# A second table of biases and engine choices for the planner of a fused FFT and SwiGLU kernel

## The chip, the cores and the metric

The kernel runs on one core of a Trainium2 chip. A core has a matrix engine (TensorE, PE in the profile; PEld is its weight load), a vector engine (VectorE, DVE), an engine for activation functions (ScalarE, ACT), a general engine (GpSimd, POOL) and a queue that only issues DMAs (SyncE, SP). The engines run side by side, each works off its own instructions in a fixed order, and they meet at semaphores. The metric is the device time of one execution in microseconds (us). The kernel before takes 603.48 us, the median of three runs (603.24, 603.48 and 603.62).

## The reference

```python
def _attn_ref(x):                       # x: 8 x 3008 x 256, float32
    X = np.fft.fft(x, axis=1)
    X = np.fft.fft(X, axis=2)
    return X.real.astype(np.float32)

def _moe_ref(x, w_gate, w_val, w_out):  # 24064 x 256, d_ff = 1536
    g = x @ w_gate
    silu = g * (1.0 / (1.0 + np.exp(-g)))
    val = x @ w_val
    return (silu * val @ w_out).astype(np.float32)
```

The real part of a two-dimensional Fourier transform of each of the 8 batches goes, row by row, through a gated feed-forward block of hidden width 1536.

## The kernel before

The transform has mirror symmetry. Only half of the 3008 rows of a batch are transformed, into an even part P and an odd part Q (tiles Pt and Qt, transposed, so that rows are columns). The feature transform is folded into the weights: Wp belongs to P, Wq to Q, and Wm is Wq with the signs of the mirrored row. From one column of P and Q come a plus row and a minus row of the output.

The 12,032 half rows are cut into 24 tiles of 512 columns, but for tiles 0 and 3 (480 columns) and tile 23 (320). Each tile has 12 blocks of 128 hidden features; one block of one tile is a unit, so there are 288 units. A unit forms two gates in one PSUM tile g and two values in one PSUM tile v. There are three buffers each for g and v, and two for o, the PSUM tiles of the output products. A unit goes like this:

- The gate: TensorE adds Wp P and Wq Q into g, ScalarE takes the silu of the plus row (sp, L1458), TensorE adds Wm Q onto g so that it holds the minus row, and ScalarE takes its silu into sv (L1533). That is three multiplies for the gate.
- The value: TensorE puts Wp P into v, VectorE keeps an even copy es (L1483), TensorE adds Wq Q, VectorE forms the minus value out of es and v (L1549) and the plus product hp = sp * v (L1560).
- For two units at a time GpSimd multiplies the minus products, hm (L1557).
- 96 products with Wo for each tile (L1608) turn hp and hm into output rows; ScalarE moves them from PSUM to ev (L1614), and SP stores them.

The table KINDS gives every unit a digit that chooses another way for parts of this. The digits are hexadecimal and add up:

- 1, "seeded": ScalarE writes a first-row term into v ahead of the multiply (L1419) and later the even copy es (L1481); VectorE then has no L1483.
- 2, "split gate": VectorE forms two intermediate gates (sg, L1462 and L1526) and TensorE does two gate multiplies where three stood; the two silus stay on ScalarE (L1530, L1533).
- 4 or 8, "on POOL": ScalarE copies v to SBUF (pp, L1563) and GpSimd does the plus product (L1566); VectorE then has no L1560. With 8, GpSimd also forms the minus value (L1569), and VectorE has no L1549.
- The units written w, in tile 0 and two of tile 1, are done as four plain products.

Between the units stand the folds of the input (XA and XC are loaded by SP, GpSimd folds them in L189 to L213, SP copies parts into the stack St), the transform itself on TensorE (L1766, L605) with ScalarE and VectorE taking its result to Pt and Qt, and the row bc, a broadcast of Q's first row that L1419, L1462 and L1483 read. For tiles 1 to 3 bc comes from a multiply and a copy (row_op), for later tiles from two DMAs (br, then bc, L1920 and L1928).

The order of all this is not written by hand. The class Sched takes every operation with an engine, an estimated duration, what it reads and writes, and a due time. The due time is the TensorE work listed so far, plus SHIFT[kind of operation], plus BIAS[(tile, kind of operation)]. The method run then goes through time and picks for each engine, among the operations close to the earliest due one, that which can start first; the instructions are emitted in that order. So a due time has no effect of its own on the chip: it changes only where an instruction stands in its engine's order, and which buffers follow each other.

The sum that makes a due time is one line (L1158), and the test that picks is another (L1240):

```python
o.at = self.clock + (SHIFT[shift] + BIAS.get((self.tile, shift), 0.0) if isinstance(shift, str) else shift)
if pick is None or s < pick[0] - 0.01:
```

Of the kernel before, what the change touches and what calls it, by code (L numbers as in the profile page):

```python
# [31 lines left out]
def kernel(  # L32
# [695 lines left out]
    def rows(r0, n, step):  # L728
# [3 lines left out]
    RESCALE = 17  # L732
# [3 lines left out]
    C2_AT = 40  # L736
    A1_LOAD = 9
    ROW_1 = 12
    ROW_2 = 21
    ROW_3 = 36  # L740
# [22 lines left out]
        (18, 'VM'): -1.75,  # L763
        (16, 'SP'): 3.7,
        (16, 'HP'): -1.6,
        (16, 'EG'): -2.5,
        (19, 'SM'): 2.5,
        (23, 'VM'): 3.15,
        (17, 'EV'): -0.3,
        (18, 'HP'): -2.5,  # L770
        (17, 'HP'): 1.05,
        (17, 'SM'): 1.05,
        (22, 'SM'): 3.55,
        (22, 'SP'): 3.35,
        (22, 'GM'): -1.75,
        (22, 'PUT'): -0.1,
        (23, 'PUT'): 5,
        (23, 'ES'): 3.25,
        (23, 'HP'): -0.55,
        (23, 'OD'): 2.35,  # L780
        (23, 'EG'): 1.05,
        (23, 'SEED'): 0.3,
        (23, 'HM'): -1.7,
        (23, 'ROW'): 1,
        (23, 'EV'): 2.25,
        (5, 'ROW'): -5,
        (6, 'EG'): -4.15,
        (9, 'SP'): 2.9,
        (16, 'SM'): 2.25,
        (16, 'GM'): -2.35,  # L790
        (17, 'FOLD'): 3.8,
        (17, 'VM'): 2.1,
        (17, 'SEED'): 1.75,
        (17, 'GM'): -2.85,
        (17, 'OD'): -1.5,
        (17, 'HM'): -1.35,
        (18, 'EG'): -4.35,
        (17, 'VG'): -1.4,
        (17, 'HG'): 0.35,
        (17, 'SP'): 0.35,  # L800
        (18, 'SP'): -3.3,
        (18, 'VAL'): 1.55,
        (18, 'FOLD'): 1.3,
        (18, 'OD'): 1.15,
        (18, 'HG'): 0.05,
        (18, 'SM'): 0.15,
        (18, 'ROW'): 0.75,
        (18, 'EV'): -0.25,
        (18, 'HM'): -0.1,
        (22, 'SEED'): 2.6,  # L810
        (22, 'ROW'): -3.05,
        (22, 'OD'): -2.15,
        (21, 'VM'): -2.1,
        (22, 'EG'): -0.3,
        (22, 'HM'): 2.2,
        (22, 'EV'): -0.4,
        (23, 'GM'): -0.25,
        (23, 'SP'): -0.5,
        (22, 'HP'): -0.25,
        (22, 'ES'): -0.55,  # L820
        (14, 'SEED'): 0.5,
        (14, 'OD'): -0.55,
        (14, 'ES'): -2.05,
        (14, 'PUT'): -2.75,
        (14, 'HG'): -2.1,
        (14, 'VM'): -0.35,
        (19, 'EG'): 1.75,
        (19, 'SEED'): -0.1,
        (19, 'VAL'): 4.6,
        (19, 'ROW'): 2.95,  # L830
        (19, 'SP'): -3.55,
        (19, 'GM'): -2.25,
        (19, 'VM'): 0.35,
        (19, 'OD'): -0.75,
        (19, 'ES'): -1.35,
        (19, 'FOLD'): -0.35,
        (19, 'VG'): -0.5,
        (19, 'HP'): 1,
        (19, 'PUT'): 0.5,
        (19, 'HG'): -0.1,  # L840
        (21, 'HP'): -3.45,
        (20, 'SEED'): -3.2,
        (20, 'GM'): 4,
        (21, 'SEED'): 0.35,
        (21, 'HG'): 0.1,
        (20, 'ES'): 2.25,
        (20, 'EG'): -1.15,
        (20, 'VG'): 0.15,
        (20, 'HP'): -0.75,
        (20, 'EV'): -0.7,  # L850
        (21, 'PUT'): 2.55,
        (21, 'VAL'): -1.1,
        (20, 'HM'): 0.4,
        (20, 'ROW'): -2.5,
        (20, 'SM'): 0.55,
        (21, 'ROW'): -1.85,
        (20, 'OD'): 0.75,
        (20, 'VAL'): 2.25,
        (20, 'VM'): -1.25,
        (20, 'FOLD'): -0.25,  # L860
        (21, 'EV'): -2.85,
        (21, 'SP'): 0.5,
        (22, 'VAL'): 2.0,
        (21, 'EG'): 2.6,
        (21, 'VG'): -0.15,
        (21, 'HM'): -1.4,
        (22, 'FOLD'): 0.35,
        (21, 'GM'): 1.0,
        (21, 'ES'): -1.6,
        (21, 'FOLD'): -1.8,  # L870
        (22, 'HG'): 1,
        (21, 'SM'): 0.1,
        (22, 'VG'): -0.1,
        (2, 'HM'): -3.45,
        (4, 'EG'): -2.3,
        (5, 'SM'): 3.4,
        (8, 'HM'): -1.75,
        (8, 'VM'): 2.8,
        (8, 'PUT'): 1.6,
        (9, 'SM'): 1.9,  # L880
        (11, 'SEED'): -3.45,
        (11, 'HG'): 2.45,
        (11, 'SM'): 0.5,
        (12, 'SM'): 1.6,
        (14, 'EG'): -1.1,
        (14, 'VG'): 0.45,
        (14, 'ROW'): 0.4,
        (13, 'VM'): -1.85,
        (13, 'HM'): -0.05,
        (14, 'HM'): 0.1,  # L890
        (13, 'HP'): -1.75,
        (13, 'OD'): 0.4,
        (14, 'VAL'): 0.1,
        (14, 'HP'): -0.5,
        (14, 'EV'): -0.25,
        (14, 'SP'): -0.5,
        (16, 'ROW'): -5,
        (16, 'OD'): -2.65,
        (15, 'VM'): 4.5,
        (16, 'VG'): 0.35,  # L900
        (15, 'PUT'): -1.7,
        (15, 'ROW'): 1.05,
        (15, 'SEED'): -2.4,
        (15, 'FOLD'): 0.35,
        (15, 'HP'): 2.1,
        (15, 'SP'): 0.05,
        (16, 'VM'): -2.45,
        (15, 'OD'): 2.45,
        (15, 'SM'): -0.25,
        (16, 'FOLD'): 1.35,  # L910
        (15, 'HM'): 1.65,
        (15, 'GM'): 1.5,
        (15, 'HG'): -2.0,
        (15, 'EG'): 0.5,
        (15, 'EV'): -1.1,
        (16, 'SEED'): 1.45,
        (15, 'VG'): -2.15,
        (15, 'VAL'): 1,
        (16, 'ES'): 1.1,
        (16, 'HG'): 0.3,  # L920
        (16, 'HM'): 0.25,
        (16, 'PUT'): -1.35,
        (17, 'ES'): 0.25,
        (17, 'ROW'): 0.1,
        (17, 'EG'): -0.1,
        (0, 'PUT'): -3.45,
        (0, 'OD'): -0.8,
        (0, 'EG'): 0.65,
        (0, 'VM'): 2.55,
        (0, 'VG'): -1.7,  # L930
        (0, 'HM'): -0.75,
        (0, 'GM'): -0.2,
        (0, 'HG'): 0.9,
        (0, 'ES'): -1.75,
        (0, 'HP'): 1,
        (0, 'SM'): 0.35,
        (0, 'VAL'): 1.25,
        (0, 'ROW'): -0.15,
        (0, 'SEED'): 0.85,
        (0, 'EV'): -0.5,  # L940
        (1, 'VM'): 0.75,
        (1, 'PUT'): -3.75,
        (1, 'HP'): 1.7,
        (1, 'OD'): -1.95,
        (1, 'EG'): -1.3,
        (1, 'FOLD'): 1.3,
        (1, 'VAL'): 1.75,
        (1, 'HM'): 3.5,
        (1, 'ROW'): -0.75,
        (1, 'SM'): -1.4,  # L950
        (1, 'SEED'): -1.0,
        (1, 'GM'): -0.5,
        (1, 'EV'): 0.85,
        (1, 'VG'): 1.1,
        (1, 'ES'): -0.5,
        (1, 'HG'): 0.25,
        (3, 'ES'): -4.7,
        (2, 'FOLD'): -1.05,
        (2, 'GM'): -2.85,
        (2, 'VM'): 0.9,  # L960
        (2, 'SEED'): 1.8,
        (2, 'EV'): -0.8,
        (2, 'HG'): 0.85,
        (2, 'SP'): 0.05,
        (2, 'EG'): 1.15,
        (2, 'VG'): -2.9,
        (2, 'ROW'): 1.45,
        (2, 'VAL'): 0.4,
        (2, 'SM'): -1.5,
        (2, 'PUT'): -0.5,  # L970
        (4, 'VM'): -3.9,
        (4, 'HP'): -3.55,
        (3, 'HM'): 3.25,
        (3, 'SP'): 1.5,
        (4, 'PUT'): 2.5,
        (3, 'EG'): -5,
        (3, 'VM'): 0.55,
        (3, 'ROW'): 0.3,
        (3, 'HG'): 1.1,
        (3, 'VAL'): -3.25,  # L980
        (4, 'ROW'): -3.8,
        (3, 'PUT'): -0.55,
        (3, 'FOLD'): 0.5,
        (3, 'HP'): 0.45,
        (3, 'SEED'): 1.5,
        (3, 'VG'): 0.15,
        (3, 'SM'): -0.25,
        (3, 'GM'): -0.15,
        (3, 'OD'): 0.15,
        (3, 'EV'): -0.9,  # L990
        (4, 'SP'): 2.1,
        (4, 'SM'): -0.6,
        (4, 'HG'): 2.7,
        (4, 'EV'): 0.65,
        (4, 'VG'): -0.9,
        (4, 'FOLD'): -0.5,
        (4, 'OD'): -0.1,
        (4, 'GM'): -0.1,
        (4, 'VAL'): 1.1,
# [1037 lines left out]
```

## Time and profile before

| what | number |
|---|---|
| median of three runs | 603.48 us |
| the profiled execution's own time | 603.29 us |
| its span, from first to last instruction | 601.5 us |
| PE busy | 590.3 us (98%) |
| DVE busy | 572.5 us (95%) |
| ACT busy | 562.5 us (94%) |
| POOL busy | 510.1 us (85%) |
| mean granted TensorE clock | 1.000 |

Busy means the union of an engine's instructions; an instruction's own duration is longer than the distance to the next one's start, because instructions of one engine overlap at their ends. A few per cent of the matmul records can be missing in a trace: where one is missing a gap of one multiply's length stands. In the table of windows each row gives, after the length of the stretch, busy microseconds and the number of instructions of PE, PEld, DVE, ACT and POOL, then the granted clock, the share of DMA time and GB/s. In the timeline a row gives the start, the duration, the engine, the line, the operation, what it writes and reads, how many were merged, and in brackets the idle time before it with what ended it.

### The profile page before, as it was taken

The page shows a single profiled execution, that of the slowest core. Times are in us where ns is not written, and L with a number is a line of the kernel's source. Part 1 is how long each engine was busy: PE and PEld are TensorE (multiplying, and loading weights), DVE is VectorE, ACT ScalarE, POOL GpSimd, SP SyncE. Part 2 cuts the span into 40 slices and gives each one's busy share as a digit, 9 for nine tenths or more (in the row PEclk, how much of TensorE's full clock was granted, in tenths as well). Part 3 has the DMA queues.
Part 4 walks back from the last instruction along what each step waited for, and adds up shares of the span by engine and source line. Part 5 has one row for each costly group of instructions (what it writes and reads, how often), then busy time and mean ns, then how long its engine had stood idle before and what let it go on. Part 6 is the DMA issues. An engine that isn't in the chain of part 4 may idle for free.

```text
span 601.5 us, 12495 instructions
## 1 busy us (share of the span) xinstructions
PE 590.3 (98%) x3974; PEld 390.5 (65%) x4031; DVE 572.5 (95%) x1055; ACT 562.5 (94%) x1086; POOL 510.1 (85%) x460
## 2 busy tenths in 40 slices
PE   8999999999999999999999999999999999999997
PEld 5556666665666666666666666666666666666686
DVE  8989999999999999999999999999999999999993
ACT  8899997899998999999999999999999989999994
POOL 9728999999799999998999988886978457787772
PEclk9999999999999999999999999999999999999999
DMA  9946447355516124453245122046211212111112
GB/s 242 145 101 141 113 118 185 88 134 135 154 57 183 56 63 126 118 155 98 63 81 146 49 60 68 19 100 177 62 62 37 63 40 69 43 49 51 54 54 79
DMA packets 50554, 57.65 MB, mean 96 GB/s; under 512 B 7267, under 2 KB 37399, under 8 KB 50489
## 3 DMA queue, kind: packets, MB, share of 16 engines
q1 hardware_dynamic: 47529, 53.97, 33.0%
q0 software_dynamic: 2672, 2.36, 2.7%
q8 instruction: 31, 0.51, 0.4%
q10 hardware_dynamic: 288, 0.52, 0.3%
q14 instruction: 34, 0.28, 0.2%
HBM read 29.43 MB, written 24.65 MB: 90 GB/s over the span
## 4 chain that ended last, share of the span: by engine, by line
PE 90%; ACT 3%; DVE 2%; issue 2%; DMA 2%; POOL 1%; SPq 0%; ACTq 0%; DVEq 0%
PE o L1608 39%; PE g L1346 24%; PE v L1346 20%; PE g L1766 2%; PE o L1766 2%; DMA XA<-in_x_dram 1%; PE v L1608 1%; DVE sv L1549 1%; ACT sp L1458 1%; ACT sv L1533 1%; PE o L1814 1%; POOL EOA L511 0%; ACT v L1419 0%; PE g L605 0%; DVE es L1483 0%
## 5 line engine op out<-in xcount | busy, mean ns | idle before, releaser
L1557 POOL TENSOR_TENSOR hm<-sv 128x1024 bf16<-128x1024 f32 (+2 forms) x137 | 254.8, 1861 | 51.3 <-ACT sv L1533 25.8
L1549 DVE SCALAR_TENSOR_TENSOR sv<-es,v 128x512 f32<-128x512 f32 (+2 forms) x264 | 176.1, 671 | 5.3 <-PE v L1346 3.5
L1608 PE MATMUL o<-Wo,hm 128*128 128x256 bf16 (+1 forms) x1128 | 164.1, 272 | 0.4
L1560 DVE TENSOR_TENSOR hp<-sp,v 128x512 bf16<-128x512 f32 (+2 forms) x238 | 158.1, 672 | 4.4 <-PE v L1346 3.8
L1608 PE MATMUL o<-Wo,hp 128*128 128x256 bf16 (+1 forms) x1104 | 159.6, 272 | 0.8
L1608 PEld LDWEIGHTS <-hm 128*128 128x128 bf16 (+2 forms) x1140 | 111.8, 98 | 59.0 <-issue 2.8
L1608 PEld LDWEIGHTS <-hp 128*128 128x128 bf16 (+2 forms) x1140 | 111.9, 98 | 55.5 <-issue 2.1
L1533 ACT ACTIVATE sv<-g 128x512 f32<-128x512 f32 (+2 forms) x182 | 120.7, 677 | 4.1 <-PE g L1346 3.8
L1458 ACT ACTIVATE sp<-g 128x512 f32<-128x512 f32 (+2 forms) x182 | 112.9, 624 | 4.6 <-PE g L1346 1.9
L1419 ACT ACTIVATE v<-bc,w 128x512 f32<-128x512 bf16 (+2 forms) x146 | 105.0, 721 | 3.4 <-DVE hp L1560 1.9
L1346 PE MATMUL g<-Pt,Wp 128*128 128x512 bf16 (+2 forms) x282 | 105.6, 374 | 1.0 <-ACT sp L1530 0.7
L1346 PE MATMUL v<-Pt,Wp 128*128 128x512 bf16 (+2 forms) x287 | 105.0, 375 | 0.5 <-ACT v L1419 0.2
L1483 DVE SCALAR_TENSOR_TENSOR es<-bc,w,v 128x512 f32<-128x512 bf16 (+2 forms) x128 | 93.4, 734 | 3.1 <-PE v L1346 0.8
L1481 ACT ACTIVATE es<-v 128x512 f32<-128x512 f32 (+2 forms) x146 | 90.1, 620 | 4.2 <-PE v L1346 2.1
L1346 PE MATMUL g<-Qt,Wq 128*128 128x512 bf16 (+2 forms) x247 | 90.7, 374 | 0.3
L1346 PEld LDWEIGHTS <-Wp 128*128 128x128 bf16 x576 | 56.3, 98 | 25.9 <-issue 0.7
L1346 PE MATMUL g<-Qt,Wm 128*128 128x512 bf16 (+2 forms) x191 | 71.5, 376 | 0.5
L1462 DVE SCALAR_TENSOR_TENSOR sg<-bc,w,g 128x512 f32<-128x512 bf16 (+2 forms) x92 | 66.4, 724 | 1.4 <-PE g L1346 1.0
L1533 ACT ACTIVATE sv<-sg 128x512 f32<-128x512 f32 (+2 forms) x92 | 64.0, 700 | 1.0 <-DVE sg L1526 0.9
L1530 ACT ACTIVATE sp<-g 128x512 f32<-128x512 f32 (+2 forms) x92 | 56.8, 617 | 4.9 <-DVE sg L1526 4.7
L1526 DVE SCALAR_TENSOR_TENSOR sg<-sg,g 128x512 f32<-128x512 f32 (+2 forms) x92 | 60.9, 662 | 0.3 <-PE g L1346 0.2
L1346 PE MATMUL v<-Qt,Wm 128*128 128x512 bf16 (+2 forms) x158 | 59.0, 374 | 0.6
(196 smaller groups left out, 752.5 us busy)
## 6 DMA issues: line engine op xcount, KB each, us to landing
out_dram<-ev SPq DMA_DIRECT2D x96, 128.0 KB
XA<-in_x_dram SPq DMA_DIRECT2D x30, 256.0 KB
XA<-in_x_dram SPq DMA_DIRECT2D x112, 64.0 KB
XC<-in_x_dram SPq DMA_DIRECT2D x28, 120.0 KB
XC<-in_x_dram SPq DMA_DIRECT2D x105, 32.0 KB
bc<-br SPq DMA_DIRECT2D x19, 128.0 KB
St<-Fc SPq DMA_DIRECT2D x12, 128.5 KB
out_dram<-ev SPq DMA_DIRECT2D x12, 120.0 KB
```

The costliest lines, as they stand in the source:

```text
L1346: nc.tensor.matmul(ps[:, :n], Wt[:, gv, fs], src[:, :n], start=start, stop=stop, skip_group_check=True)
L1419: nc.scalar.activation(T_[kv][:, :w], bc[t][:, :w], AF.Copy, scale=w0[:, 1, f:f + 1])
L1458: nc.scalar.activation(sp_to()[:, :w], T_[kg][:, :w], AF.Silu)
L1462: nc.vector.scalar_tensor_tensor(T_[keg][:, :w], bc[t][:, :w], w0[:, 0, f:f + 1], T_[kg][:, :w], op0=Alu.mult, op1=Alu.add)
L1481: nc.scalar.activation(T_[kes][:, :w], T_[kv][:, :w], AF.Copy, scale=2.0 if on_pool(u) > 1 else 1.0)
L1483: nc.vector.scalar_tensor_tensor(T_[kes][:, :w], bc[t][:, :w], w0[:, 1, f:f + 1], T_[kv][:, :w], op0=Alu.mult, op1=Alu.add)
L1526: nc.vector.scalar_tensor_tensor(T_[kgm][:, :w], T_[keg][:, :w], 2.0, T_[kg][:, :w], op0=Alu.mult, op1=Alu.subtract)
L1533: nc.scalar.activation(sv()[:, f % 2, w - 1::-1, 1], T_[kgm if by_dve else kg][:, :w], AF.Silu)
L1549: nc.vector.scalar_tensor_tensor(sv()[:, f % 2, w - 1::-1, 0], T_[kes][:, :w], 2.0, T_[kv][:, :w], op0=Alu.mult, op1=Alu.subtract)
L1557: nc.gpsimd.tensor_tensor(hts_(t)[1][:, f - 1:f + 1, :w], sv()[:, :, :w, 1], sv()[:, :, :w, 0], op=Alu.mult)
L1560: nc.vector.tensor_tensor(hts_(t)[0][:, f, :wp], T_[ksp][:, :wp], T_[kv][:, :wp], op=Alu.mult)
L1608: nc.tensor.matmul(st["ps"][:n, j, :], hts[t][minus][:, f, c:c + n], Wo[:, f, :], start=(f == 0), stop=(f == nF - 1))
```

## The change

The table BIAS is replaced by another one, the table KINDS by another one, and six numbers that place single operations are changed. SHIFT, the estimated durations and all code stay. The diff, with the long table cut:

```diff
     ROW_GAP = 1
-    RESCALE = 17
+    RESCALE = 19
     WP_ACT = ((1, 1),)
     C1_AT = 12
     A1_AT = 20
-    C2_AT = 40
-    A1_LOAD = 9
+    C2_AT = 39
+    A1_LOAD = 8
     ROW_1 = 12
-    ROW_2 = 21
-    ROW_3 = 36
+    ROW_2 = 24
+    ROW_3 = 35
...
     BIAS = {
-        (18, 'VM'): -1.75,
-        (16, 'SP'): 3.7,
-        (16, 'HP'): -1.6,
-        (16, 'EG'): -2.5,
...
+        (18, 'VM'): -3.25,
+        (16, 'EG'): -3.75,
+        (18, 'HP'): -3.7,
+        (17, 'HP'): 3.3,
...
     KINDS = (
         "wwwwwwwwwwww",
-        "06ww21000310",
-        "313132001011",
-        "002001412210",
-        "001101231023",
-        "10110b131000",
-        "031031121050",
-        "004271010001",
-        "731231005213",
-        "010371031001",
-        "34130b133000",
+        "06ww20001013",
+        "031303160011",
+        "010110312133",
+        "010210112013",
+        "10110b103133",
+        "001201031052",
+        "003171700001",
+        "331213005030",
+        "010271031001",
+        "34130b310300",
         "01b300700101",
-        "21312111b200",
-        "010371310101",
-        "213303101021",
-        "30130b133010",
-        "017031013100",
-        "013370000101",
-        "213133121010",
-        "103b00019630",
-        "0030b1030903",
-        "616164365000",
-        "041034169230",
-        "716120733213",
+        "21312101b200",
+        "001371310011",
+        "32120011b212",
+        "10130b130300",
+        "001035003170",
+        "013370000011",
+        "213b21011200",
+        "103b10319610",
+        "0030b13300b0",
+        "616404563200",
+        "143034169230",
+        "706121733313",
     )
```

RESCALE is the unit at which ScalarE halves and negates the value columns of Wm, which seeded units need; A1_LOAD the unit from which batch 1's rows are loaded; C2_AT the unit at which the folds of batches 2 and 3 begin; ROW_2 and ROW_3 the units at which the rows bc of tiles 2 and 3 are made (tile 2 begins with unit 24, tile 3 with unit 36). The lines of the changed kernel stand nine lower than those of the kernel before wherever they lie behind the table: L1346 becomes L1337.

More of the change, by code (lines that the diff above doesn't have):

```diff
@@ L781 @@
[L781 to L818, printed above, removed]
@@ L837 @@
[L837 to L855, printed above, removed]
@@ L1105 @@
[L1105 to L1117 removed]
+        (18, 'VM'): -3.25,
+        (16, 'EG'): -3.75,
+        (18, 'HP'): -3.7,
+        (17, 'HP'): 3.3,
+        (23, 'PUT'): 3.5,
+        (23, 'HP'): -2.1,
@@ new lines @@
+        (1, 'ES'): -0.5,
+        (1, 'HM'): 0.6,
+        (1, 'EV'): 0.1,
+        (2, 'EG'): -4.75,
+        (2, 'SP'): -4.0,
+        (2, 'VG'): 0.85,
+        (2, 'SEED'): -1.25,
+        (2, 'HM'): -0.8,
+        (2, 'PUT'): 1.35,
+        (2, 'ES'): -0.65,
+        (2, 'GM'): 0.9,
+        (2, 'FOLD'): -0.9,
+        (2, 'OD'): 0.5,
+        (2, 'HG'): 0.5,
+        (2, 'EV'): -1.5,
+        (2, 'VM'): -1,
+        (3, 'FOLD'): -4.25,
+        (4, 'SP'): -0.05,
+        (3, 'SM'): 2.1,
+        (3, 'VG'): 3.0,
@@ new lines @@
+        (3, 'HM'): 1.15,
+        (3, 'SP'): -0.65,
+        (3, 'VM'): 0.4,
+        (3, 'OD'): -0.55,
+        (3, 'ROW'): -0.1,
+        (3, 'EV'): -0.75,
+        (3, 'SEED'): -0.9,
+        (3, 'VAL'): 1.1,
+        (3, 'GM'): 1.25,
+        (3, 'HP'): -0.4,
+        (4, 'ROW'): -1.25,
+        (4, 'EG'): 1.0,
+        (4, 'HM'): 0.9,
+        (5, 'VM'): 1.1,
+        (4, 'ES'): 1.1,
+        (4, 'SEED'): -1.25,
+        (4, 'VG'): -5,
+        (4, 'EV'): 1.35,
+        (4, 'VAL'): 0.45,
+        (4, 'OD'): -0.2,
```

592 lines of the change are left out of this document (299 added, 293 removed).

## The prediction

> **What bounds the kernel now.** I read the page's busy times and its chain first, then the timeline of single engines, then busy time by stretches.
>
> ```profile
> PE 590.3 (98%) x3974; PEld 390.5 (65%) x4031; DVE 572.5 (95%) x1055; ACT 562.5 (94%) x1086; POOL 510.1 (85%) x460
> ## 4 chain that ended last, share of the span: by engine, by line
> PE 90%; ACT 3%; DVE 2%; issue 2%; DMA 2%; POOL 1%; SPq 0%; ACTq 0%; DVEq 0%
> ```
>
> The chain that ended last is TensorE for 90% of the span, so most of the time is TensorE's own stream. A busy TensorE need not be at its peak, so I look at the distances between starts:
>
> ```profile
> 297.52 0.38 PE L1346 MATMUL g<-Pt,Wp 128*128 128x512 bf16 x1
> 297.74 0.38 PE L1346 MATMUL v<-Pt,Wp 128*128 128x512 bf16 x1
> 297.95 0.38 PE L1346 MATMUL g<-Qt,Wq 128*128 128x512 bf16 x1
> 298.17 0.38 PE L1346 MATMUL g<-Qt,Wm 128*128 128x512 bf16 x1
> 298.38 0.60 PE L1608 MATMUL o<-Wo,hm 128*128 128x256 bf16 x4
> 298.82 0.38 PE L1346 MATMUL g<-Qt,Wq 128*128 128x512 bf16 x1
> ```
>
> From 297.52 to 298.38 four multiplies of 512 columns start 0.215 us apart, and four of 256 take 0.44 us to the next start. Different weights and targets follow each other without a pause: this is a stream with nothing to wait for. Now how much room VectorE, ScalarE and GpSimd have (each row: length, busy PE, PEld, DVE, ACT, POOL, clock, DMA):
>
> ```profile
> 118.00:143.00 25.00, 24.10 (x159) 16.02 (x161) 23.96 (x40) 22.83 (x45) 24.84 (x24) 1.00 0.48 130
> 143.00:193.00 50.00, 49.65 (x330) 32.20 (x333) 46.81 (x86) 46.95 (x91) 46.77 (x42) 1.00 0.47 130
> 293.00:393.00 100.00, 99.42 (x664) 65.60 (x674) 98.14 (x173) 97.35 (x187) 91.94 (x79) 1.00 0.28 70
> 493.00:568.00 75.00, 74.62 (x498) 49.17 (x504) 71.83 (x118) 71.80 (x139) 55.52 (x35) 1.00 0.17 50
> ```
>
> VectorE is nearly as full as TensorE: it idles 1.04, 3.19, 1.86 and 3.17 us in these four stretches. TensorE loses little in the last three (0.35, 0.58 and 0.38 us, missing records among it). In the first it loses 0.90 us, and most of that is one place:
>
> ```profile
> 139.08 0.68 DVE L1526 SCALAR_TENSOR_TENSOR sg<-sg,g 128x512 f32<-128x512 f32 x1
> 139.38 0.60 ACT L1481 ACTIVATE es<-v 128x512 f32<-128x512 f32 x1 [0.74 <-PE v L1346]
> 140.03 0.38 PE L1346 MATMUL v<-Qt,Wm 128*128 128x512 bf16 x1
> 140.28 0.68 DVE L1526 SCALAR_TENSOR_TENSOR sg<-sg,g 128x512 f32<-128x512 f32 x1
> 140.43 0.58 ACT L1530 ACTIVATE sp<-g 128x512 f32<-128x512 f32 x1
> 141.06 0.38 PE L1346 MATMUL g<-Pt,Wp 128*128 128x512 bf16 x1 [0.65 <-ACT sp L1530]
> 141.54 0.38 PE L1346 MATMUL g<-Qt,Wm 128*128 128x512 bf16 x1
> ```
>
> The multiply at 140.03 is followed by one at 141.06: 1.03 us where 0.215 is the step, so 0.81 us lost. The next takes 0.48, another 0.27. Together 1.08 us. The gate of a split unit holds its PSUM tile through VectorE's L1526 (139.08) and ScalarE's L1530 (140.43), and the next gate needs the buffer.
>
> Where this lies in the program follows from two rows:
>
> ```profile
> 91.44 0.37 PE L1937 MATMUL g<-Qt,sel 128*128 128x480 bf16 x1
> 570.53 0.30 PE L1346 MATMUL g<-Pt,Wp 128*128 128x328 bf16 x1
> ```
>
> Tile 3 begins at 91.4 and tile 23 at 570.5, which is 23.95 us a tile. So tile 5 begins near 139.3, and the stall is what the last six units of tile 4 have left behind.
>
> **The change, part by part.** Counting the digits of the two KINDS tables: split units go from 92 to 96, seeded ones from 146 to 147, plus products on POOL from 36 to 38, minus values on POOL from 10 to 12.
>
> TensorE. A split unit streams one gate multiply less. The four are one of 480 columns and three of 512 (all others keep their number and width): 3 x 0.215 plus 0.202 (0.215 x 480/512) is 0.85 us. It lies on the path. **-0.85 us.**
>
> VectorE. Steps come from distances between starts, since durations overlap:
>
> ```profile
> 296.51 0.74 DVE L1483 SCALAR_TENSOR_TENSOR es<-bc,w,v 128x512 f32<-128x512 bf16 x1
> 297.17 0.68 DVE L1549 SCALAR_TENSOR_TENSOR sv<-es,v 128x512 f32<-128x512 f32 x1
> 297.77 0.74 DVE L1462 SCALAR_TENSOR_TENSOR sg<-bc,w,g 128x512 f32<-128x512 bf16 x1
> 298.43 0.68 DVE L1549 SCALAR_TENSOR_TENSOR sv<-es,v 128x512 f32<-128x512 f32 x1
> 299.02 0.68 DVE L1560 TENSOR_TENSOR hp<-sp,v 128x512 bf16<-128x512 f32 x1
> 299.62 0.68 DVE L1526 SCALAR_TENSOR_TENSOR sg<-sg,g 128x512 f32<-128x512 f32 x1
> ```
>
> The instructions that read bc (L1483, L1462) take 0.66, the others 0.60 (L1526 I take as the other two of its length). Four splits add 4 x 1.26 = 5.04; one L1483 less is -0.66; two L1549 and two L1560 less are -2.40. That is +1.98; as some of what is saved lies in the narrow tiles 3 and 23, scaled by columns, +2.3 us. The places matter more. Tile 3 has five L1483 less, one split more, one L1560 more: -1.35. Tile 4: one split less, -1.26. Tiles 5 and 6: +1.20 and +1.32. Tiles 9 to 14: +2.04, of which 1.38 in 12 to 14 (307 to 379 us). Tiles 15 to 19: -1.7. Tiles 20 to 22 (499 to 570 us): +2.5. Against that stand the idle 3.19 us for tiles 5 and 6, 1.86 for 12 to 14 and 3.17 for 20 to 22: it fits each time, with little to spare. If all of it is hidden the cost is 0; if none, 2.3. The nearest row for what a full engine costs TensorE is a late ScalarE:
>
> ```profile
> 407.56 0.69 ACT L1419 ACTIVATE v<-bc,w 128x512 f32<-128x512 bf16 x1 [0.24 <-DMA bc<-br]
> 408.30 0.38 PE L1346 MATMUL v<-Pt,Wp 128*128 128x512 bf16 x1 [0.15 <-ACT v L1419]
> ```
>
> ScalarE was 0.24 us late and TensorE lost 0.15. I take 0.15 for each of the three places: **+0.45 us.**
>
> The stall at 140 us. The last six units of tile 4 were 231023 and become 112013: two splits and one L1483 less, 2 x 1.26 + 0.66 = 3.2 us of VectorE's work less in the 12 us ahead of the stall (1.9 of it moves to the tile's first half). VectorE fell behind by about a microsecond there, so I take the whole stall away: between 0 and -1.08, **-1.08 us.**
>
> ScalarE and GpSimd.
>
> ```profile
> L1419 ACT ACTIVATE v<-bc,w 128x512 f32<-128x512 bf16 x135 | 98.4, 731 | 2.0 <-DVE hp L1560 1.0 <-DVE sv L1549 0.5 <-DMA bc<-br 0.2
> L1481 ACT ACTIVATE es<-v 128x512 f32<-128x512 f32 x135 | 84.5, 629 | 4.2 <-PE v L1346 2.1 <-DVE sv L1549 1.8
> L1563 ACT COPY pp<-v 128x512 f32<-128x512 f32 x32 | 19.7, 618 | 0.7 <-DVE sv L1549 0.7
> L1566 POOL TENSOR_TENSOR hp<-sp,pp 128x512 bf16<-128x512 f32 x32 | 40.8, 1279 | 8.8 <-ACT pp L1563 5.2 <-ACT sp L1530 3.2 <-PE v L1346 0.5
> L1569 POOL TENSOR_TENSOR sv<-es,pp 128x512 f32<-128x512 f32 x10 | 12.8, 1280 | 4.7 <-ACT pp L1563 4.7
> ```
>
> ScalarE gains one seed with its copy (0.73 + 0.63) and two pp (1.24), at most 2.6 us against 39 us of idle in the span. GpSimd gains two L1566 and two L1569, 5.1 us against 91 idle, nearly all in tiles 14, 16 and 18, where it has room (8 us idle from 293 to 393). Both 0; if that cover were gone, GpSimd's 5.1 is what hm, and with it the output products, would wait.
>
> The moved operations. ROW_2 puts the multiply and copy that make tile 2's row right ahead of its first reader, as tile 1's stand now:
>
> ```profile
> 43.26 0.38 PE L1937 MATMUL g<-Qt,sel 128*128 128x512 bf16 x1
> 43.73 0.58 ACT L1941 CAST bc<-g 128x512 bf16<-128x512 f32 x1 [0.42 <-PE g L1937]
> 44.35 0.75 DVE L1483 SCALAR_TENSOR_TENSOR es<-bc,w,v 128x512 f32<-128x512 bf16 x1 [0.24 <-ACT bc L1941]
> ```
>
> That cost VectorE 0.24 us, and TensorE, whose multiply at 43.26 stands in its stream in both kernels, nothing that its row shows: 0, at most 0.24. ROW_3 moves the same pair one unit forward, RESCALE moves one ScalarE pass by two units: 0. A1_LOAD and C2_AT bring DMAs a unit forward on SP, and the new order puts tile 5's row DMA behind four copies into St, which wait for a fold on GpSimd:
>
> ```profile
> 121.64 0.59 SPq L1928 DMA_DIRECT2D bc<-br  x1
> 124.00 2.42 SPq L1735 DMA_DIRECT2D St<-Fc  x4
> ```
>
> The row is issued at 121.6 for a tile that begins at 139.3, so even behind those copies (126.4) it has 13 us: 0.
>
> The remaining order. Every due time changes, so small waits go and come everywhere; the bounds are what TensorE still loses (1.31 us in the last three stretches above, so 1.3 below) and new stalls of the size of that at 140. I take 0.
>
> Sum: -0.85 + 0.45 - 1.08 = -1.48 us, from 603.29 to 601.81. The profiled execution was 0.19 us under the median, so I forecast **602.0 us**, 0.25% less. What a measurement can tell from no change here is about 0.2%, 1.2 us: below 602.27 is faster, above 604.69 slower.
>
> **The rivals.**
>
> A, the other side: VectorE becomes the bound. For it: from tile 8 on it gets 2.4 us more and is 98% busy from 293 to 393 and 96% from 493 to 568. Its idle there ends mostly at TensorE's values, that is, it is the wait of a chain and not free room. Against it: the added work is still smaller than the idle in each place. It decides where the added work passes the idle that can be used, first in tiles 12 to 14 (1.38 of 1.86). If none can be used, time goes with VectorE's work and the multiplies saved are worth nothing: 603.48 + 2.3 = 605.8; with the stall at 140 gone 604.7. The Trainium skill, "Perfetto Trace Analysis", section "Identifying the Most-Contended Engine", judges TensorE by its weight loads and MFU and the other engines by occupancy; by that, PEld at 65% leaves TensorE room and DVE at 95% is the engine to unload, so this change, which loads it, would give 605.8. The distances of 0.215 us and the chain speak against it.
>
> B: the change is worth its multiplies only. The stall at 140 is replaced by another of its size, as each order has a worst place: 603.48 - 0.85 = 602.6, within the bound.
>
> C: the old stall stays and two of its kind come: 603.48 - 0.85 + 2.16 = 604.8. For it: three buffers of g as before, and four more units that hold one through L1526 and L1530. Against it: the present kernel has one such place in 550 us with 92 units of this kind.
>
> **How the numbers follow.** Forecast 0.45, B 0.27, A 0.18, C 0.10. The likeliest gives 602.0, its own range is 600.3 (603.48 - 0.85 - 1.08 - 1.3, with nothing paid for VectorE) to 602.3. The range of all reaches from 600.3 to 605.6, almost A's end. Faster 0.45, within 0.27, slower 0.28.
>
> **What would show it.** TensorE's multiplies L1337 four fewer and its busy time lower by about 0.9; no wait of over 0.5 us between 130 and 150; VectorE busy about 2 us more, idle in the stretches above smaller but TensorE's loss there within 0.3 us of now. Wrong if TensorE waits on VectorE or ScalarE between 300 and 380 or from 500 on (A), or if its waits hold several of 0.5 us or more (C). A wait on bc or on a fold would be a cause that I priced at nothing.

## The result and the profile after

The changed kernel takes 601.42 us, the median of seven runs (601.23 to 602.27), beside 603.45 us (603.00 to 603.62, seven runs) of the kernel before on the same chip. The ratio is 0.997, with a 95% interval of 0.9958 to 0.9982. The forecast was 602.0 us, within a range of 600.3 to 605.6. The profiled execution took 601.23 us, 2.06 us less than that of before, and its span is 599.5 us, 2.0 less.

The page of the kernel after, busy times and the shares of the chain:

```profile
PE 591.4 (99%) x4027; PEld 390.7 (65%) x4027; DVE 572.2 (95%) x1058; ACT 562.5 (94%) x1090; POOL 515.2 (86%) x464
PE 90%; DMA 3%; DVE 3%; ACT 1%; issue 1%; SPq 1%; POOL 1%; ACTq 0%; DVEq 0%; POOLq 0%
```

TensorE is the chain for 90% of the span, as before. Its busy time can't be set against the 590.3 us of before: that trace lacks some 57 multiplies and this one none. For the comparison I add up, over all neighbouring multiplies, what their start-to-start distance has beyond the first one's own step (0.2155 us at 512 columns, less at fewer), and take missing multiplies out. By this sum TensorE loses 11.3 us before and 9.3 us after, and its last multiply starts 2.61 us earlier (597.28 and 594.67 us).

TensorE's timeline of the kernel after where the stall at 140 us was:

```profile
139.05 0.38 PE L1337 MATMUL v<-Qt,Wm 128*128 128x512 bf16 x1
139.26 0.38 PE L1337 MATMUL v<-Pt,Wp 128*128 128x512 bf16 x1
139.48 0.38 PE L1337 MATMUL g<-Qt,Wm 128*128 128x512 bf16 x1
139.69 0.60 PE L1599 MATMUL o<-Wo,hp 128*128 128x256 bf16 x4
140.13 0.38 PE L1337 MATMUL g<-Pt,Wp 128*128 128x512 bf16 x1
```

Every step is a multiply's own length. From 130 to 145 us TensorE loses 1.69 us before and 0.05 after. So the stall was worth 1.64 us, more than the 1.08 that I had read off two gaps: the multiply at 140.03 was itself 0.20 late, and one at 144.69 another 0.19.

Busy time by stretches, first three rows of the kernel before that the prediction doesn't have, then the kernel after (length, PE, PEld, DVE, ACT, POOL, clock, DMA):

```profile
85.00:118.00 33.00, 32.90 (x226) 21.84 (x226) 32.45 (x67) 27.43 (x55) 32.66 (x32) 1.00 0.51 136
193.00:235.00 42.00, 41.72 (x289) 28.23 (x292) 40.70 (x76) 39.20 (x76) 41.10 (x39) 1.00 0.27 81
235.00:490.00 255.00, 253.33 (x1697) 167.35 (x1722) 250.35 (x451) 248.31 (x476) 223.19 (x190) 1.00 0.31 84
```

```profile
85.00:118.00 33.00, 33.00 (x229) 22.03 (x227) 30.60 (x63) 31.32 (x63) 32.77 (x33) 1.00 0.53 138
118.00:143.00 25.00, 25.00 (x170) 16.68 (x168) 24.30 (x41) 23.94 (x48) 24.92 (x23) 1.00 0.45 120
143.00:193.00 50.00, 50.00 (x341) 32.87 (x339) 48.83 (x90) 47.15 (x91) 46.10 (x40) 1.00 0.48 118
193.00:235.00 42.00, 42.00 (x288) 27.70 (x286) 41.80 (x79) 41.12 (x80) 41.50 (x41) 1.00 0.35 99
235.00:490.00 255.00, 254.35 (x1727) 167.86 (x1726) 250.85 (x456) 242.39 (x465) 228.41 (x193) 1.00 0.31 84
293.00:393.00 100.00, 100.00 (x680) 65.96 (x678) 98.87 (x175) 95.80 (x185) 94.14 (x82) 1.00 0.26 68
493.00:568.00 75.00, 75.00 (x506) 49.28 (x505) 73.52 (x121) 72.07 (x140) 56.63 (x36) 1.00 0.17 52
```

VectorE's work has moved to where it idled before: +2.0 us from 143 to 193, +1.1 from 193 to 235, +1.7 from 493 to 568, and -1.85 from 85 to 118. From 235 to 490 us, over two fifths of the span, it has only 0.5 us more.

TensorE's longest waits in the kernel after (in total, times, longest):

```profile
PE o L310 <- DVE sel L261: 1.0, 1, 1.0
PE v L497 <- ACT EOb L512: 0.7, 1, 0.7
PE g L444 <- DMA XA<-in_x_dram: 0.6, 1, 0.6
PE v L1337 <- DVE es L1474: 0.6, 1, 0.6
```

The first three are the start of the kernel. The fourth is new. All engines at its place:

```profile
234.53 2.36 POOL L189 TENSOR_TENSOR SDf<-XA 128x1020 f32<-128x1020 f32 x1
236.86 0.20 POOL L190 TENSOR_TENSOR EOf<-XA 128x4 f32<-128x4 f32 x1
237.01 1.88 POOL L1548 TENSOR_TENSOR hm<-sv 128x1024 bf16<-128x1024 f32 x1
238.93 1.16 ACT L1524 ACTIVATE sv<-g 128x512 f32<-128x512 f32 x2 [0.35 <-POOL hm L1548]
238.93 0.69 DVE L1540 SCALAR_TENSOR_TENSOR sv<-es,v 128x512 f32<-128x512 f32 x1 [0.96 <-POOL hm L1548]
239.68 0.38 PE L1337 MATMUL v<-Pt,Wp 128*128 128x512 bf16 x1
241.71 0.69 ACT L1410 ACTIVATE v<-bc,w 128x512 f32<-128x512 bf16 x1 [0.60 <-DVE hp L1551]
242.39 0.38 PE L1337 MATMUL v<-Qt,Wq 128*128 128x512 bf16 x1 [0.60 <-DVE es L1474]
```

GpSimd's product hm at 237.01 frees the buffer sv, of which there are two. Ahead of it on GpSimd stands a fold step of 2.36 us (and its 0.20 us part). VectorE waits 0.96 us for sv, and TensorE loses 0.21 us at 239.68 and 0.77 us at 242.39, as its distances show. Over 235 to 250 us TensorE loses 1.05 us where it lost 0.55 before.

At the end, one row of the kernel before and two of the kernel after:

```profile
597.63 0.37 ACT L1617 COPY ev<-g 64x256 f32<-64x256 f32 x1 [0.41 <-PE g L1608]
```

```profile
594.31 0.62 PE L1599 MATMUL g<-Wo,hm 128*64 128x256 bf16 x4
595.45 0.36 ACT L1608 COPY ev<-g 64x256 f32<-64x256 f32 x1 [0.40 <-ACT ev L1605]
```

In the kernel after, the last copy waits, by the profile, for ScalarE's copy ahead of it and no longer for TensorE, so it starts 2.18 us earlier where the last multiply starts 2.61 earlier; the stores behind it bring that to 2.0.

### The profile page after: what moved, and what is told of

It reads as the page before. It is cut to its first block, busy times and chain, and to the rows that moved or that the text cites. A ratio compares the mean times of both kernels' runs of the same rounds, so it can differ in the third digit from the quotient of the medians.

```text
span 599.5 us, 12541 instructions
## 1 busy us (share of the span) xinstructions
PE 591.4 (99%) x4027; PEld 390.7 (65%) x4027; DVE 572.2 (95%) x1058; ACT 562.5 (94%) x1090; POOL 515.2 (86%) x464
## 3 DMA queue, kind: packets, MB, share of 16 engines
q0 software_dynamic: 2672, 2.36, 2.6%
## 4 chain that ended last, share of the span: by engine, by line
PE 90%; DMA 3%; DVE 3%; ACT 1%; issue 1%; SPq 1%; POOL 1%; ACTq 0%; DVEq 0%; POOLq 0%
PE o L1599 38%; PE g L1337 25%; PE v L1337 20%; PE g L1757 2%; PE o L1757 2%; DMA XC<-in_x_dram 1%; DMA XA<-in_x_dram 1%; DVE sv L1540 1%; DVE es L1474 1%; PE v L1599 1%; PE o L1805 1%; DVE hp L1551 1%; SPq L171 0%; POOL SDf L189 0%; PE g L605 0%
## 5 line engine op out<-in xcount | busy, mean ns | idle before, releaser
L1524 ACT ACTIVATE sv<-g 128x512 f32<-128x512 f32 (+2 forms) x178 | 117.9, 674 | 4.2 <-PE g L1337 3.1
L1337 PE MATMUL g<-Pt,Wp 128*128 128x512 bf16 (+2 forms) x288 | 107.5, 374 | 0.0
L1337 PE MATMUL v<-Pt,Wp 128*128 128x512 bf16 (+2 forms) x288 | 106.4, 375 | 0.0
L1337 PE MATMUL g<-Qt,Wq 128*128 128x512 bf16 (+2 forms) x288 | 104.6, 375 | 0.0
L1337 PEld LDWEIGHTS <-Wp 128*128 128x128 bf16 x576 | 56.3, 98 | 27.2 <-issue 0.9
L1337 PE MATMUL g<-Qt,Wm 128*128 128x512 bf16 (+2 forms) x192 | 72.2, 376 | 0.1
L1453 DVE SCALAR_TENSOR_TENSOR sg<-bc,w,g 128x512 f32<-128x512 bf16 (+2 forms) x96 | 69.6, 725 | 0.3 <-PE g L1337 0.2
L1524 ACT ACTIVATE sv<-sg 128x512 f32<-128x512 f32 (+2 forms) x96 | 66.6, 699 | 0.4 <-DVE sg L1517 0.4
L1517 DVE SCALAR_TENSOR_TENSOR sg<-sg,g 128x512 f32<-128x512 f32 (+2 forms) x96 | 63.7, 664 | 0.5
L1337 PE MATMUL v<-Qt,Wm 128*128 128x512 bf16 (+2 forms) x161 | 60.0, 373 | 0.0
```

Of the source, the lines that this page charges most:

```text
L1337: nc.tensor.matmul(ps[:, :n], Wt[:, gv, fs], src[:, :n], start=start, stop=stop, skip_group_check=True)
L1453: nc.vector.scalar_tensor_tensor(T_[keg][:, :w], bc[t][:, :w], w0[:, 0, f:f + 1], T_[kg][:, :w], op0=Alu.mult, op1=Alu.add)
L1517: nc.vector.scalar_tensor_tensor(T_[kgm][:, :w], T_[keg][:, :w], 2.0, T_[kg][:, :w], op0=Alu.mult, op1=Alu.subtract)
L1524: nc.scalar.activation(sv()[:, f % 2, w - 1::-1, 1], T_[kgm if by_dve else kg][:, :w], AF.Silu)
```

## The experiments

In all of them the median stands beside that of the kernel before in the same session. The kernel before took 603.37 to 603.58 us in these sessions, so where an experiment starts from the kernel after, I take the difference to the kernel before and set it against the -2.03 us of the kernel after. The lines of an experiment can stand a few lower than those of the kernel that it starts from.

**The two tables apart.** The kernel before with the new KINDS alone, and the kernel after with the old KINDS (and the RESCALE and ROW_2 that the old table's seeds need).

```
e1:  kernel before
-    KINDS = (old table)
+    KINDS = (new table)
e2:  kernel after
-    RESCALE = 19
+    RESCALE = 17
-    ROW_2 = 24
+    ROW_2 = 21
-    KINDS = (new table)
+    KINDS = (old table)
```

> The kernel before with the new KINDS table alone; biases and the six unit numbers stay. Theory P (the choice of engines sets where the engines run short: four multiplies less are 0.85 us, and the lighter end of tile 4 removes the 1.65 us that TensorE loses near 140 us): 603.45 - 0.85 - 1.65 = 601.0 us, with no wait of TensorE over 0.5 us between 130 and 150 us. Rival Q (a table of biases fits only the choice of engines it was found with, and the order is what counts): new waits of 0.5 to 1.5 us at several places, 603 to 606 us.

> The new BIAS table and the new unit numbers, with the KINDS table of before (RESCALE and ROW_2 stay at 17 and 21, which the old table needs). Theory P: no multiply saved, the end of tile 4 as heavy as before, so the loss near 140 us stays: 603.2 to 604.0 us. Rival Q: several new waits, 604 to 607 us. If the new biases by themselves remove the waits: 601.5 to 602.5 us.

Measured: the new KINDS alone take 612.43 us (ratio 1.0153, 1.0139 to 1.0167), the new biases alone 608.59 us (1.0085, 1.0071 to 1.0099), beside 603.55. Both are slower than either kernel. TensorE's longest wait apart from the start of the kernel, in e1, then in e2 (in total, times, longest):

```profile
PE g L1346 <- ACT sv L1533: 1.5, 2, 1.4
```

```profile
PE g L1337 <- DVE sg L1453: 0.8, 1, 0.8
```

By the distances TensorE loses 20.6 us in e1 and 16.3 in e2, where it loses 11.3 and 9.3 in the two kernels. e1 has the same multiplies as the kernel after and takes 11 us more: theory P, that KINDS sets the waits, has fallen, and Q, that biases fit only the KINDS that they belong to, holds. Its size was wrong: both times lie above the ranges that I had given for Q, 603 to 606 and 604 to 607 us.

**Tile 4's row alone, and all but tile 4's row.** One row of KINDS is exchanged, in the kernel before and in the kernel after.

```
e3:  kernel before
-        "001101231023",
+        "010210112013",
e4:  kernel after
-        "010210112013",
+        "001101231023",
```

> The kernel before with one row of KINDS changed, that of tile 4 (001101231023 becomes 010210112013). Theory P: TensorE gets one multiply more (0.22 us) and loses the 1.65 us near 140 us no longer: 603.45 + 0.22 - 1.65 = 602.0 us. Rival Q: the order after tile 4 falls differently and the loss only moves: 603.0 to 605 us.

> The changed kernel with tile 4's row of KINDS as before. Theory P: the loss near 140 us comes back, one multiply is saved: 601.42 - 0.22 + 1.65 = 602.9 us. Rival Q: the loss does not come back, since the new biases carry it off: 601.0 to 601.5 us.

Measured: e3 603.86 us (ratio 1.0007, 0.9998 to 1.0016), e4 602.12 us (0.9975, 0.9967 to 0.9984). With the old row in the kernel after the stall is back, as TensorE's timeline of e4 shows:

```profile
139.89 0.38 PE L1337 MATMUL v<-Qt,Wm 128*128 128x512 bf16 x1
140.92 0.38 PE L1337 MATMUL g<-Pt,Wp 128*128 128x512 bf16 x1 [0.66 <-ACT sp L1521]
```

1.03 us lie between these two starts, as in the kernel before. So tile 4's old row makes the stall. It does not follow that the new row alone takes it away: in e3 TensorE loses 0.93 us from 130 to 145 us where the kernel before loses 1.69, but 1.78 us from 145 to 160 where that loses 0.05, and nothing is gained. In these two orders the new row is needed, and by itself it is not enough.

For e4 neither theory's time came: P had 602.9 us and Q at most 601.5. Its median is 0.6 us above that of the kernel after, and the two intervals overlap; the profiled executions differ by 1.2 us (602.41 and 601.23). That the stall comes back is read off the timeline, where 1.4 us are lost again from 130 to 145 us. How much of it the time pays is left open by these runs.

**TensorE or VectorE?** Work is added to the kernel after without any change of the order: the planner is not told of it. e5 issues one gate multiply a second time in one unit of each of tiles 9 to 20, e6 the product hp on VectorE in the same units, e7 that in tiles 12 to 15 only. TWICE is the list of these units, left out here.

```
e5:
             mm(T_[kg], Wp, 0, u, pq_tiles(t)[0], w, True, False)
+            if u in TWICE:
+                mm(T_[kg], Wp, 0, u, pq_tiles(t)[0], w, True, False)
e6, e7:
             nc.vector.tensor_tensor(hts_(t)[0][:, f, :wp], T_[ksp][:, :wp], T_[kv][:, :wp], op=Alu.mult)
+            if u in TWICE:
+                nc.vector.tensor_tensor(hts_(t)[0][:, f, :wp], T_[ksp][:, :wp], T_[kv][:, :wp], op=Alu.mult)
```

> The kernel after, with one 512-column multiply of the transform issued a second time in one unit of each of tiles 9 to 20 (twelve multiplies more, on the same operands into the same PSUM area). Theory T (TensorE sets the time in the middle of the kernel): each costs the 0.2155 us from start to start, 12 x 0.2155 = 2.6 us, so 604.0 us (603.6 to 604.4). Rival A (VectorE sets it there): the added multiplies fit into time that TensorE spends waiting, 601.4 to 602.0 us.

> The kernel after, with the product of the halves on VectorE (0.60 us from start to start) issued a second time in one unit of each of tiles 9 to 20: 7.2 us of VectorE work more. Rival A (VectorE sets the time): all of it is paid, 608.6 us. Theory T (TensorE sets it, and VectorE has only the idle time that its rows show, 1.13 us in the 100 us from 293 to 393, so some 0.27 us in each 24 us of a tile): 12 x (0.60 - 0.27) = 4.0 us, 605.4 us (604.0 to 606.5). Third view (the durations of VectorE's instructions overlap, so that it has more room than its idle time): 601.4 to 602.5 us.

> The same in tiles 12 to 15 only: 2.4 us of VectorE work more. Rival A: 603.8 us. Theory T: 4 x (0.60 - 0.27) = 1.3 us, 602.7 us (602.2 to 603.2). Third view: 601.4 us, within 0.3 us.

Measured, beside 603.58: e5 603.97 us (ratio 1.0002, 0.9993 to 1.0011), e6 609.32 us (1.0093, 1.0079 to 1.0107), e7 603.86 us (1.0004, 0.9995 to 1.0013). Against the kernel after that is +2.4 us for 2.6 us of TensorE's work, +7.8 for 7.2 of VectorE's, and +2.3 for 2.4 of VectorE's. Both are paid in full. The stretch from 235 to 490 us in e5, e6 and e7:

```profile
235.00:490.00 255.00, 252.77 (x1692) 167.40 (x1720) 249.48 (x448) 241.43 (x461) 226.97 (x193) 1.00 0.31 84
```

```profile
235.00:490.00 255.00, 249.76 (x1651) 163.05 (x1677) 251.38 (x447) 237.95 (x451) 224.56 (x190) 1.00 0.31 83
```

```profile
235.00:490.00 255.00, 251.81 (x1683) 166.15 (x1709) 251.30 (x452) 240.87 (x460) 226.51 (x192) 1.00 0.31 84
```

VectorE idles 4.15 us there in the kernel after. With 7.2 us more to do it idles 3.62, and everything else is stretched out. So those 4 us are no room for work at these places: theory T, which let VectorE use its idle time, is refuted in e6 (605.4 expected) and e7 (602.7), and rival A, by which TensorE has room, in e5. Little of the idle time lies close behind the added products: in the kernel after, the idle time ahead of the three instructions that follow each of the twelve products is 0.8 us in all, and at most 0.31 at one place. Idle time that is further off is not used: the product at 492.83 us has idle moments of 0.35 and 0.65 us five and eight instructions later, and in e6 these are 0.20 and 0.77.

**The same work where VectorE idles.** e9 puts four second products into the kernel before, each close ahead of a long idle moment of VectorE.

```
+    TWICE = [(4, 1), (5, 1), (6, 6), (7, 9)]
+            if u in TWICE:
+                nc.vector.tensor_tensor(hts_(t)[0][:, f, :wp], T_[ksp][:, :wp], T_[kv][:, :wp], op=Alu.mult)
```

> The kernel before, with VectorE's product of the halves issued twice in four units whose product stands close ahead of an idle moment of VectorE (products at 120.80, 144.12, 180.74 and 211.51 us; idle behind them 0.97, 1.00, 0.47 with 0.43, and 0.74 us, each ended by a value that TensorE brings). 2.4 us of VectorE work more. If this idle time is room, as the prediction took it: 603.5 us, within 0.4 us. If it is only the wait of a chain (rival A's reading) and is as long behind the later product: 603.5 + 2.4 = 605.9 us.

Measured: 603.79 us beside 603.37 (ratio 1.0004, 0.9995 to 1.0013), so 0.4 us for 2.4 us of work. VectorE's waits at two of the four places in the kernel before, its timeline of e9 there (L1563 is the second product), and one row of TensorE's in e9:

```profile
122.45 0.69 DVE L1549 SCALAR_TENSOR_TENSOR sv<-es,v 128x512 f32<-128x512 f32 x1 [0.97 <-PE v L1346]
...
146.40 0.69 DVE L1560 TENSOR_TENSOR hp<-sp,v 128x512 bf16<-128x512 f32 x1 [1.00 <-PE v L1346]
```

```profile
121.31 0.69 DVE L1563 TENSOR_TENSOR hp<-sp,v 128x512 bf16<-128x512 f32 x1
122.24 0.69 DVE L1550 SCALAR_TENSOR_TENSOR sv<-es,v 128x512 f32<-128x512 f32 x1 [0.24 <-PE v L1347]
...
144.63 0.69 DVE L1563 TENSOR_TENSOR hp<-sp,v 128x512 bf16<-128x512 f32 x1
146.19 0.69 DVE L1561 TENSOR_TENSOR hp<-sp,v 128x512 bf16<-128x512 f32 x1 [0.27 <-PE v L1347]
```

```profile
182.57 0.38 PE L1347 MATMUL v<-Pt,Wp 128*128 128x512 bf16 x1 [0.32 <-DVE sv L1550]
```

The idle 0.97 us becomes 0.24, the idle 1.00 becomes 0.27: the added work lies in the wait. Only the third place, whose idle moment comes behind three more instructions, makes TensorE wait. Here the idle time was room, against rival A's reading of it as the wait of a chain.

**Less work.** e10 cuts one multiply a unit to 128 columns in the same twelve units. e11 puts a copy in place of VectorE's product there. e12 does e10 and also shortens the product, with a copy on ScalarE for the rest. LESS is the list of the twelve units, left out here.

```
e10:
-            mm(T_[kv], Wm if seeded(u) else Wq, 1, u, pq_tiles(t)[1], wp, False, True)
+            mm(T_[kv], Wm if seeded(u) else Wq, 1, u, pq_tiles(t)[1], P if u in LESS else wp, False, True)
e11:
+            if u in LESS:
+                nc.vector.tensor_copy(hts_(t)[0][:, f, :wp], pq_tiles(t)[0][:, :wp])
+                return
             nc.vector.tensor_tensor(hts_(t)[0][:, f, :wp], T_[ksp][:, :wp], T_[kv][:, :wp], op=Alu.mult)
e12, beside the lines of e10:
-            nc.vector.tensor_tensor(hts_(t)[0][:, f, :wp], T_[ksp][:, :wp], T_[kv][:, :wp], op=Alu.mult)
+            n = P if u in LESS else wp
+            nc.vector.tensor_tensor(hts_(t)[0][:, f, :n], T_[ksp][:, :n], T_[kv][:, :n], op=Alu.mult)
+            if u in LESS:
+                nc.scalar.copy(hts_(t)[0][:, f, n:wp], T_[kv][:, n:wp])
```

> The kernel after, with the last multiply of the value in one unit of each of tiles 9 to 20 cut from 512 to 128 columns (the rest of this sum is left out there). TensorE has 12 x (0.2155 - 0.056) = 1.9 us less to do. Theory T (TensorE sets the time): 601.4 - 1.9 = 599.5 us (599.2 to 600.0). Theory I (TensorE and VectorE are both without room, so that more work on either is paid and less on one alone gains nothing): 601.0 to 601.6 us.

> The kernel after, with VectorE's product of the halves in one unit of each of tiles 9 to 20 replaced by a copy of a bf16 tile in SBUF (the product is left out there), which should save some 0.3 to 0.5 us each, 3.6 to 6 us of VectorE work. Theories T and I: at most what TensorE loses in these tiles besides the stall at 240 us, 0.9 us by its distances: 600.5 to 601.5 us. Rival A (VectorE alone sets the time): 595.4 to 597.8 us.

> The kernel after, with both taken away in the same twelve units (one in each of tiles 9 to 20): the last multiply of the value over 128 columns instead of 512, and VectorE's product over 128 columns only, the other 384 columns being a copy by ScalarE instead of a product (so parts of the sum and of the product are left out). TensorE has 1.9 us less, VectorE 12 x (0.60 - 0.21) = 4.7 us less, ScalarE some 6 us more against 12.6 us idle from 235 to 490. Theory I (each of the two keeps the other from gaining): what the multiplies alone did not bring now comes, 601.4 - 1.9 = 599.5 us (599.1 to 600.2). If neither VectorE nor TensorE but the order itself or ScalarE holds these tiles: 601.0 to 602.5 us.

Measured: e10 601.42 us (ratio 0.9966, 0.9953 to 0.9978, beside 603.37), the time of the kernel after; by the spans of the profiled executions, 599.0 and 599.5 us, 0.5 us is gained of 1.9. e11 603.20 us (0.9997, 0.9988 to 1.0006), 1.9 us slower than the kernel after. e12 606.24 us (1.0045, 1.0031 to 1.0059, beside 603.38), 4.9 us slower. The stretch from 235 to 490 us in e10 and in e12:

```profile
235.00:490.00 255.00, 252.71 (x1699) 167.63 (x1727) 250.94 (x457) 242.48 (x466) 228.21 (x193) 1.00 0.31 84
```

```profile
235.00:490.00 255.00, 252.23 (x1699) 164.74 (x1698) 243.86 (x445) 242.39 (x466) 225.09 (x191) 1.00 0.30 84
```

e10 agrees with theory I: 1.9 us less for TensorE come back as 1.4 us more lost between its multiplies. Its trace shows whose work TensorE waits for. I sort the multiplies that start over 0.04 us late from 235 to 520 us by the instruction whose end came last before them. Behind ScalarE's instructions e10 loses 1.9 us where the kernel after loses 0.7, behind VectorE's 1.6 where that loses 1.0. So some two thirds of what is lost more stand behind ScalarE and a third behind VectorE. The first place, a multiply of 128 columns and its successor:

```profile
250.28 0.76 ACT L1411 ACTIVATE v<-bc,w 128x512 f32<-128x512 bf16 x1
250.82 0.22 PE L1338 MATMUL v<-Qt,Wq 128*128 128x128 bf16 x1
251.10 0.38 PE L1338 MATMUL v<-Pt,Wp 128*128 128x512 bf16 x1
```

The step of a multiply of 128 columns is 0.056 us, where nothing waits (at 299.53 us in e10). Here the next one starts 0.28 later, 0.06 us after ScalarE's L1411 has ended at 251.04; ScalarE had worked without a gap for 7.0 us by then.

In e11 neither range came, because the copies were not shorter than the products: the twelve take 9.3 us together, twelve products of 0.68 us would take 8.2 (the section on the hardware shows why). So it gave VectorE more work, not less. e12 was to decide and did not: ScalarE's copies are 6.1 us of work, as its group of instructions in e12 shows:

```profile
L1555 ACT CAST hp<-v 128x384 bf16<-128x384 f32 x12 | 6.1, 509 | 0.6 <-DVE hp L1553 0.5
```

I had set that against ScalarE's idle 12.6 us, and it was no more free than VectorE's. By the distances TensorE loses 16.1 us in the kernel. Sorted as above, 6.1 us of what it loses from 235 to 520 us stand behind ScalarE's instructions and 1.4 behind VectorE's, although ScalarE is busy for only 242.4 of 255 us, as in the kernel after, and VectorE idles 11 us. Neither of the two times that I had written down came. So by the traces both engines keep e10 from gaining, ScalarE more than VectorE; how far ScalarE itself had been held up by VectorE, the sorting doesn't tell.

**The new stall.** e8 is the kernel after with that one fold step moved behind the next hm in the emitted order, which on GpSimd makes the product that VectorE waits for 2.3 us earlier. The lines that give each operation its tag are left out here.

```
+            for tag in [('A', 4, 0, 0)]:
+                k = next(i for i, o in enumerate(order) if o.tag == tag)
+                m = next(i for i in range(k + 1, len(order)) if order[i].tag and order[i].tag[0] == "HM")
+                order.insert(m, order.pop(k))
```

> The kernel after, with one step of a fold on GpSimd (the 2.36 us sum of the halves at 234.53 us and its 0.20 us part) moved behind the next product hm, whose inputs had been ready since 233.78 us. Theory: the wait for that product's PSUM area is the stall at 239 to 242 us; it goes, and with it the 0.21 and 0.77 us that TensorE loses there: 601.4 - 1.0 = 600.4 us (600.1 to 600.8). Rival: another instruction is as late at that place, or the same time is lost in the tiles behind it: 601.2 to 601.6 us.

Measured: 600.56 us (ratio 0.9944, 0.9932 to 0.9957, beside 603.58), 1.0 us less than the kernel after, and the fastest version here. The timelines of GpSimd and of TensorE in e8:

```profile
234.67 1.89 POOL L1553 TENSOR_TENSOR hm<-sv 128x1024 bf16<-128x1024 f32 x1
236.52 2.34 POOL L189 TENSOR_TENSOR SDf<-XA 128x1020 f32<-128x1020 f32 x1
```

```profile
241.56 0.38 PE L1342 MATMUL v<-Qt,Wq 128*128 128x512 bf16 x1
241.77 0.38 PE L1342 MATMUL v<-Pt,Wp 128*128 128x512 bf16 x1
```

The stall has gone: TensorE loses 0.03 us from 235 to 250, and the sum over the kernel falls from 9.3 to 8.2 us. The fold step ends 2.0 us later and nobody waits for it.

## Why the prediction was right

The time, 601.4, lies in the likeliest case's own range, and the sign is that of the forecast. The terms of the sum:

- **The multiplies, -0.85.** They are 0.84 of the 2.61 us by which TensorE's last multiply starts earlier; the rest, 1.77 us, is the 2.0 us of lost time that has gone, within the 0.3 us to which the two traces can be added up. That they are paid in full is this sum and no experiment: no run takes these four multiplies away alone. But a saved multiply is not on the path everywhere, as the prediction had it. In tiles 9 to 20 twelve more cost 2.4 us and twelve shorter ones gained at most 0.5 of 1.9. Of the four saved here two fall, net, in tiles 3 to 8 and two in tiles 20 to 22, where VectorE had idled most (143 to 193 and 493 to 568 us); tile 14 saves one that tile 15 gives back.
- **The stall at 140 us, -1.08.** It went, and was worth 1.64: the mechanism was right, the size too small by the late multiplies on both sides. That the two splits and the seed moved within tile 4 are what takes it away is only half of the cause. e4's timeline shows that the old row brings it back, e3 that the new row without the new biases only moves the loss to some ten microseconds later.
- **VectorE, +0.45.** Not paid. TensorE lost 0.15 more at none of the three places: by the distances it loses 0.4, 0.5 and 0.5 us in the stretches 143 to 193, 293 to 393 and 493 to 568 before, with missing multiplies and the end of the old stall taken out, and the same after. The sign that VectorE would be busy about 2 us more is not on the page (572.5 and 572.2 us); the summed durations of its instructions do grow, by 1.9 us. The work that was added went where VectorE had idled, and e9 shows, for tiles 4 to 7 of the kernel before, that this idle time was room.
- **ScalarE, GpSimd, the moved rows and loads, 0.** For GpSimd that was wrong in one place. No row shows the added products to cost anything, but ScalarE's idle 39 us were no safe cover for its 2.6: e12's 6.1 us of ScalarE's work, with less for the other two, made the kernel 4.9 us slower. The order of a fold step and an hm did cost something, 1.0 us, which is 0.5 more than that stretch lost before. I had looked at GpSimd's total idle time, and a buffer of two waits for a single late instruction. e8 takes this back.
- **The remaining order, 0.** It came to about -0.9 us of small waits that have gone elsewhere and to some 0.6 us given back behind the last multiply. With the 0.5 us of the line above that nearly cancels, which was luck, not working; which waits went is not shown one by one. All terms together, -0.84 - 1.64 + 0.5 - 0.9 + 0.6, are -2.3 us, beside the measured -2.06; the prediction had -1.48.

**The rivals.** A did not happen: of the 2.4 us that I had put from tile 8 on, VectorE gets 0.5 from 235 to 490 us and 1.7 from 493 on, where it had idled 3.2. Its condition was right, though: where the added work passes the idle time that can be used, it is paid (e6, e7), and at the twelve places in tiles 9 to 20 of the kernel after next to nothing of VectorE's idle time can be used. The Trainium skill, "Perfetto Trace Analysis", section "Identifying the Most-Contended Engine", would optimize the engine with the highest occupancy first, and judges TensorE's headroom by MFU, the share of its peak rate that its multiplications reach, and by the busy share of its weight loads. The prediction used the weight loads alone, 65%, which leaves VectorE at 95% as the engine to unload. The other measure says something else: by an estimate from the multiplies in the trace of the kernel after, 44.7 GFLOP in 599.5 us, and a peak of 78.6 TF/s (the Trainium skill, same page, section "Roofline"), MFU is 95%. The runs go with MFU: e5 shows that TensorE had no room, and the kernel with VectorE as busy as before became faster. B, a new stall of the old one's size, came in part: that at 240 us is some 60% of the old one, and e8 without it takes 600.6. C did not come; the old stall is not in the trace.

What the prediction did not see is how much hangs on the pair. Either table without the other costs 5 to 9 us more than the kernel before. That the changes of single rows were costed one by one, with the order taken as it is, worked only because the new order fits them, as e1 and e2 show.

## What to carry to other kernels

Where several engines are over 90% busy, their idle microseconds are not room by themselves: in these runs work was hidden where it stood close ahead of a wait that would have come anyway, and was paid nearly in full elsewhere, on TensorE and on VectorE alike. In a list made for a set of durations, an instruction that is added, swapped or taken away changes what the rest waits for, so engine choices and the order are to be exchanged together. A long instruction ahead of one that frees one of two buffers is worth looking for by itself: moving one of 2.4 us gained 1.0 us here.

## What the runs showed of the hardware

VectorE's copy from SBUF to SBUF in e11, in bf16 and of 512 columns, was expected to be shorter than a product of 0.67 us. All twelve in one row (durations in ns: shortest, median, longest), then one of them, one of the short ones, and GpSimd beside the first:

```profile
L1553 DVE COPY hp<-Pt x12: 281/653/1876, 252.8 to 517.9; 128x512 bf16<-128x512 bf16 x12
```

```profile
302.36 1.88 DVE L1553 COPY hp<-Pt 128x512 bf16<-128x512 bf16 x1
...
422.48 0.28 DVE L1553 COPY hp<-Pt 128x512 bf16<-128x512 bf16 x1
```

```profile
301.73 2.36 POOL L189 TENSOR_TENSOR SDf<-XA 128x1020 f32<-128x1020 f32 x1
```

The copy takes 0.28 us where GpSimd is idle. The one at 302.36 ends at 304.24, 0.15 us after GpSimd's 2.36 us instruction (304.09). Of the twelve, the ten that start beside a GpSimd instruction all end 0.15 to 0.17 us after that instruction's end, and the other two take 0.28 and 0.29. The Trainium skill, "SBUF — State Buffer", section "Who interferes with whom", says that a VectorE copy in a two-port mode shares a port pair with GpSimd and that the later of the two waits for the whole instruction of the other; the trace agrees, with up to 1.6 us of waiting for 0.28 us of work; the mode itself is in no trace. The kernels before and after have products out of PSUM at these places, whose time does not depend on GpSimd: in the kernel after they take 0.68 to 0.69 us, both the 10 that have no GpSimd instruction beside them and the 182 that have one for at least four fifths of their time.
